# Transposes of the second softmax three at a time, product copies behind the next silu, two weight blocks swapped

## The chip, the cores and the metric

One core of one Trainium2 chip. The metric is device time in microseconds (us), the median of several runs. The engines are TensorE (PE, with its weight loads shown apart as PEld), VectorE (DVE), ScalarE (ACT), GpSimd (POOL) and SyncE (SP), which here issues nearly all the DMA loads and stores. Each engine works through its own list of instructions in order.

## The reference

Three layers one after the other on 4 batches of 576 tokens (2304 in all), everything in fp32: masked attention, a soft mixture of 8 experts, and a gated layer.

```python
scores = scale * q @ k.T; scores = where(mask, scores, -1e9)   # 8 heads of 64; a local or a strided mask
x = softmax(scores) @ v                       # -> x: 2304 x 512
logits = x @ phi                              # 2304 x 32 slots
slot_input = softmax(logits, over tokens).T @ x
for e in range(8):                            # 4 slots each
    slot_out[e] = relu(slot_input[e] @ w1[e]) @ w2[e]     # 512 -> 1024 -> 512
x = softmax(logits, over slots) @ slot_out    # 2304 x 512, of rank 32
g, val = x @ w_gate, x @ w_val                # 512 -> 1536
out = (silu(g) * val) @ w_out                 # 1536 -> 512
```

The weights of the gated layer come in as 64-bit floats and are turned into fp32 in the kernel.

## The kernel before

**Order.** The order of all instructions is written out by hand: what the Python code emits first for an engine runs first there. Tiles come from pools; a pool with a number of buffers hands out a buffer that is free at that point of the program, and the instruction that first writes the new tile waits for the readers of the old one. A load that SP issues also waits until the load eight places before it has landed, since eight semaphores go round.

**Attention** (to about 107 us). 16 units, a unit being one head of two batches, in 48 steps of three score blocks: scores on PE (`qk`, L296), masking and maximum on DVE (L302), exponentials on ACT (`expo`, L314), transposes (`tr`, L321, copied by ACT, L324), product with v (`pv`, L334). Keys and queries of a unit are loaded by `load_qk` (L267, L268), v by `load_v` (L274). Three units are in memory at a time: the fourth unit's keys are loaded when the first unit's scores are done (step `n == 2`).

**Weights** go through `load_half` (L178) in halves of 512 KB, in the order of the list `loads`: three units of the gated layer first (`PRE`: g0, g1, o0), then blocks of w1 (numbers 1 to 12 in the order `WORDER`) and w2 (16 to 31), 1 MB each. They lie in the pool `wp`, a ring of 14 buffers, but for a few that use other memory (0, 13, 14, 15, and the three in `SHARED`). `load_to` and the list `WTO` say how far the loads are to be after each unit. `PRECONV` lists the attention steps at which `pre` turns g0, g1 and o0 from 64-bit to 32-bit floats (ACT at L197, then DVE).

**Experts** (to 153 us). `w1_mm` multiplies the slot inputs with the w1 blocks in the order `W1ORDER`, which ends with 12 and 11, and asks for two more halves after each block: so the last eleven w2 blocks are loaded, the last of them (31) after block 12 has been multiplied and before 11 has. Then the w2 blocks follow (L745), with `hid`, the softmax over slots (`c_soft`, two parts) and its transposes (`c_tr`, eight, each three PE transposes and a DVE copy into `cs`) between them; `CTR` says behind which block how many of the transposes stand, `CTE` how many after the last.

**Gated layer** (from 153 us). Gate and value weights come in twelve units g0 to g11, output weights in six (o0 to o5), 1 MB each, into a pool of four buffers (`load_g`, L686). It lies over memory that `wp` had. Unit g2 is the first that is loaded there. A half is turned into fp32 by `half`: `prep` (ACT L227, then a clamp on POOL, L228) and three steps on DVE (L232, L236, L240). `stage` starts a half, `part` does one DVE step, and a planner spends a `room` of DVE time per step of the main loop on parts. An output unit is split into a high part (ACT copy, `split_hi`, L793) and a low part (POOL, `split_lo`, L796). For each unit f, `a_mm` multiplies the expert outputs with the gate and value weights (L805, copied by ACT), `a_st` spreads the result (L812), ACT copies it into `St[f]` (L813) and DVE subtracts in its lower half (L814). So x never has to be built: `gv` multiplies `St[f]` with `cs` for a block of 512 tokens (gate L825, value L826), ACT takes the silu (L831), DVE multiplies (L832), ACT copies the product into a rounded high part `hh` (L833), POOL subtracts for the low part `hl` (L834). Three products later (`LAG`), `omm` multiplies high and low parts with the output weights: twelve matmuls per product (L852), summed in four output banks per block and taken out by ACT (tiles 0 and 2) and DVE (1 and 3) at L875 or L878 when a group is complete. The last two token tiles are stored at L861. `HEAD` is the list of what is done ahead of the loop: `a0` and `a1` are `a_mm` of units 0 and 1, `s0` and `s1` `a_st`, `g` a `stage`, `p1` one `part`, `w1` a PE matmul that only keeps it warm.

Of the kernel before, what the change touches and what calls it, by code (L numbers as in the profile page):

```python
# [9 lines left out]
F32 = mybir.dt.float32  # L10
# [21 lines left out]
SHARED = W2ORDER[2:5]  # L32
WORDER = list(range(1, 13)) + list(W2ORDER[:2])
REST = list(W2ORDER[5:])
# [3 lines left out]
ORDER = [("g", 2), ("g", 3), ("o", 1), ("g", 4), ("g", 5), ("o", 2), ("g", 6), ("g", 7), ("o", 3), ("g", 8), ("g", 9), ("g", 10), ("g", 11), ("o", 4), ("o", 5)]  # L38
LAG = 3
WT = (0, 0)  # L40
ATDVE = ((15, 1),)
WIN1 = ((0, 3), (3, 7), (7, 10))
HID1 = 1
CTR = {9: 1, 10: 1, 11: 1, 12: 1, 13: 1}
CTE = (1,)
# [9 lines left out]
START = (2, 1)  # L55
HEAD = "a0 a1 g s0 w1 s1 p1 w1"
WARM0 = 8
# [54 lines left out]
def build(ctx: ExitStack, tc: tile.TileContext, cst, phi, qh, kh, vh, w1, w2, wgv, wo, out):  # L112
# [404 lines left out]
    with tc.manual_schedule():  # L517
# [15 lines left out]
        load_v(2)  # L533
        load_half(2)
        def cut(out, k, op, src):
# [176 lines left out]

        def c_tr(bp, b, hf):
            ps = bank("tr", 2)
            for k in range(3):
                PE.transpose(ps[:, 96 * k:96 * k + 96],
                             cst2[hf][:, k, 2 * bp + b].rearrange("p q s -> p (q s)").bitcast(F32),
                             ident[0:96, 0:96])
            DVE.tensor_copy(cs[:, 2 * bp + b, 288 * hf:288 * hf + 288], ps[:, 0:288])

        ctr = [(c_tr, (bp, b, hf)) for bp in range(2) for b in range(2) for hf in range(2)]
        while last[0] in rest:
# [19 lines left out]
        for n, j in enumerate(W2ORDER):  # L742
            e, hf = divmod(j - 16, 2)
            for k in range(4):
                PE.matmul(out=sp_[32 * k:32 * k + 32, :], lhsT=hz[:, 4 * hf + k, 32 * e:32 * e + 32],  # L745
                          rhs=wch(j, k), start=(n == 0), stop=(n == 15), skip_group_check=True)
            load_half(2)
            if n == HID1:
                hid(1)
            if n < 2:  # L750
                c_soft(n)
            if n == 2:
                sil = mid.tile([128, 1], F32, name="sil")
                ACT.activation(out=sil, in_=m_sb, func=AF.Silu)
            for _ in range(CTR.get(n, 0)):
                fn, a = ctr.pop(0)
                fn(*a)
        so = xp.tile([128, 512], F32, tag="hs", name="so")
# [62 lines left out]
        def gv(bi, f):  # L821
# [10 lines left out]
            DVE.tensor_tensor(out=h[:, 0:n], in0=pvv[:, 0:n], in1=sg[:, 0:n], op=ALU.mult)  # L832
            ACT.copy(hh[bi, f][:, 0:n], h[:, 0:n])  # L833
            POOL.tensor_tensor(out=hl[bi, f][:, 0:n], in0=h[:, 0:n], in1=hh[bi, f][:, 0:n].bitcast(F32),  # L834
                               op=ALU.subtract)

# [3 lines left out]
        def omm(p, bi, f):  # L840
# [6 lines left out]
            def mm(t, terms):  # L847
                z = len(ob[t])
                c = 512 // z
                for k, o in enumerate(ob[t]):  # L850
# [4 lines left out]
                    if last and 2 in terms:  # L855
                        if end:
# [3 lines left out]
                                              op=ALU.add)  # L860
                            SP.dma_start(out=out[r:r + 128, c * k:c * k + c], in_=tmp[:, 0:c])  # L861
                        else:
# [68 lines left out]

        split_hi(0)
        split_lo(0, 0)
        split_lo(0, 1)
        for step in HEAD.split():
# [5 lines left out]
            elif k == "g":  # L941
                stage(-2)
            elif k == "p":
                for _ in range(a):
                    part(-1)
            else:
                warm(a)
        for n in range(len(seq) + LAG):
# [17 lines left out]
            if n < len(seq):  # L966
                force(n, ("g", seq[n][2]))
                gv(*seq[n][1:])
            while staged and staged[0][0] <= n and PART <= room:
                room -= PART  # L970
                part(n)
            if n >= STG:
                stage(n)
                if n < 2 * STG:
                    stage(n)

# [19 lines left out]
```

## Time and profile before

| what | value |
|---|---|
| runs of before | 361.76 us median of 3 (359.48, 361.76, 364.25) |
| the profiled execution | 362.2 us by the clock of the runs, its span in the trace 360.4 us |
| busy share of the span | PE 94%, PEld 68%, DVE 61%, ACT 52%, POOL 37% |
| mean granted clock of PE | 0.994 of full speed |
| moved by DMA | 71.94 MB, mean 200 GB/s |

A row of the timeline gives start, duration, engine, line, operation, output and inputs, and how often; in brackets stands the idle time of the engine ahead of it and what the profile takes for its end. The number after PEclk in the view by stretches is the granted clock as a share of 2.4 GHz. PE is busy nearly everywhere, so the places where it is not are what to look for.

### The profile page before, as it was taken

Reading aid. Unit: us, or ns where it says so; the run is one execution under the profiler, and the core shown is the slowest. Engines: PE = TensorE matmul, PEld = TensorE weight load, DVE = VectorE, ACT = ScalarE, POOL = GpSimd, SP = SyncE. Lnnn points to the kernel's source line nnn. Section 1 sums busy time; section 2 is a strip of 40 time slices with the busy share of each in tenths; the row PEclk is TensorE's granted clock in tenths of the full one; section 3 lists DMA queues with packets and bytes.
Section 4 is the critical chain, followed back from the end, with each engine's and each line's share of the span. In section 5 each row is a group of like instructions: output and inputs, shape, how many; then the busy total and the mean of one; then the engine's idle time right before and its main releaser. Section 6 shows DMA issues by size and latency. Waiting matters only on the chain.

```text
span 360.4 us, 7681 instructions
## 1 busy us (share of the span) xinstructions
PE 338.7 (94%) x2856; PEld 243.9 (68%) x2856; DVE 219.4 (61%) x707; ACT 186.8 (52%) x449; POOL 132.6 (37%) x163
## 2 busy tenths in 40 slices
PE   7799989899989999978999899999998999999995
PEld 4677766787737443345777487777785787878774
DVE  4868785765546017247877788788859844142432
ACT  3877969766842003256666565465535653434321
POOL 1522323122110020036555475485525774434431
PEclk9999999999999999998999999999999999999999
DMA  7998998959998999684232542154300003030304
GB/s 212 398 400 299 348 369 322 303 201 352 341 411 303 367 409 408 254 333 172 85 127 102 161 160 73 74 198 154 116 0 2 2 2 116 0 115 4 117 30 144
DMA packets 23397, 71.94 MB, mean 200 GB/s; under 512 B 2624, under 2 KB 3520, under 8 KB 23360
## 3 DMA queue, kind: packets, MB, share of 16 engines
q1 hardware_dynamic: 23216, 71.45, 53.9%
q8 instruction: 22, 0.36, 0.4%
q14 instruction: 15, 0.12, 0.1%
q10 hardware_dynamic: 144, 0.01, 0.0%
HBM read 66.73 MB, written 4.72 MB: 198 GB/s over the span
## 4 chain that ended last, share of the span: by engine, by line
PE 75%; DMA 8%; DVE 6%; ACT 5%; issue 3%; SPq 2%; POOL 1%; DVEq 0%; ACTq 0%
PE o L852 38%; PE sc L296 5%; PE pv L334 5%; PE pv L745 4%; PE gv L825 4%; PE tr L321 3%; DMA w<-in_w 3%; PE gv L826 3%; PE tr L360 2%; PE lg L380 2%; DMA s<-in_kh 2%; PE ms L445 2%; DMA s<-in_qh 2%; DMA g<-in_wgv 1%; DVE h L832 1%
## 5 line engine op out<-in xcount | busy, mean ns | idle before, releaser
L834 POOL TENSOR_TENSOR hl<-h,hh 128x512 fp32r<-128x512 f32 (+1 forms) x60 | 71.0, 1183 | 90.7 <-ACT hh L833 90.7
L852 PE MATMUL o<-woh,hh 128*128 128x512 f32 (+1 forms) x220 | 88.2, 401 | 3.1 <-ACT acc L875 1.7
L852 PE MATMUL o<-wol,hh 128*128 128x512 f32 (+1 forms) x220 | 85.6, 390 | 0.0
L832 DVE TENSOR_TENSOR h<-gv,sg 128x512 f32<-128x512 f32 (+1 forms) x59 | 37.5, 635 | 49.8 <-ACT sg L831 40.0
L833 ACT CAST hh<-h 128x512 fp32r<-128x512 f32 (+1 forms) x60 | 34.7, 578 | 55.3 <-DVE h L832 55.3
L852 PE MATMUL o<-woh,hl 128*128 128x512 f32 (+1 forms) x220 | 59.3, 386 | 0.0
L852 PEld LDWEIGHTS o<-woh,hh 128*128 128x128 f32 x220 | 41.7, 190 | 17.8 <-DVE acc L878 3.1
L277 POOL COPY s<-s 32x390 f32<-32x390 f32 (+1 forms) x48 | 23.8, 498 | 68.4 <-DMA s<-in_vh 46.9
L831 ACT ACTIVATE sg<-gv 128x512 f32<-128x512 f32 (+1 forms) x60 | 33.4, 556 | 26.3 <-PE gv L825 26.2
L852 PEld LDWEIGHTS o<-wol,hh 128*128 128x128 f32 x220 | 41.8, 190 | 7.6
L852 PEld LDWEIGHTS o<-woh,hl 128*128 128x128 f32 x220 | 41.1, 188 | 8.6
L314 ACT ACTIVATE tmp<-tmp,mx 128x96 f32<-128x96 f32 (+1 forms) x144 | 40.8, 363 | 3.0 <-DVE mx L302 3.0
L302 DVE CUSTOM_DVE_ANT_0 tmp<-sc,s 128x96 f32<-128x96 f32 (+1 forms) x144 | 28.1, 245 | 17.6 <-PE sc L296 16.4
L296 PEld LDWEIGHTS sc<-s,s 64*64 64x64 f32 x576 | 23.1, 132 | 13.1 <-issue 7.5
L296 PE MATMUL sc<-s,s 64*64 64x96 f32 (+1 forms) x576 | 27.8, 240 | 4.5 <-DMA s<-in_kh 1.7
L324 ACT COPY tmp<-tr 96x384 f32<-96x384 f32 x47 | 20.2, 477 | 20.6 <-PE tr L321 20.5
L825 PE MATMUL gv<-cs,St 128*128 128x512 f32 (+1 forms) x60 | 25.4, 423 | 2.4 <-DVE St L814 2.4
L796 POOL TENSOR_TENSOR wol<-wo,woh 128x512 fp32r<-128x512 f32 x12 | 15.5, 1297 | 24.0 <-ACT woh L793 24.0
L334 PE MATMUL pv<-s,tmp 96*64 96x65 f32 x576 | 22.4, 225 | 0.6 <-POOL s L277 0.6
L826 PE MATMUL gv<-cs,St 128*128 128x512 f32 (+1 forms) x59 | 22.6, 383 | 0.2 <-DVE h L832 0.2
L334 PEld LDWEIGHTS pv<-s,tmp 96*64 96x64 f32 x576 | 19.0, 137 | 4.0 <-issue 0.8
L321 PE MATMUL tr<-cst_t,tmp 128*96 128x128 f32 x144 | 21.1, 280 | 0.4 <-ACT xT L361 0.4
(164 smaller groups left out, 456.6 us busy)
## 6 DMA issues: line engine op xcount, KB each, us to landing
w<-in_w SPq DMA_DIRECT2D x50, 512.0 KB, 8.4
g<-in_wgv SPq DMA_DIRECT2D x10, 1024.0 KB, 5.1
g<-in_wo SPq DMA_DIRECT2D x5, 1024.0 KB, 4.9
s<-in_vh SPq DMA_DIRECT2D x16, 292.5 KB, 6.1
out<-osb SPq DMA_DIRECT2D x17, 256.0 KB, 2.2
s<-in_qh SPq DMA_DIRECT2D x15, 288.0 KB, 6.2
s<-in_kh SPq DMA_DIRECT2D x15, 288.0 KB, 6.3
wx<-in_w SPq DMA_DIRECT2D x7, 512.0 KB, 5.1
```

Source lines behind the costliest of these rows:

```text
L296: PE.matmul(out=ps[r, W * j:W * j + W], lhsT=qt[u % AHEAD][r, 64 * i:64 * i + 64], rhs=kt[u % AHEAD][r, c0:c0 + W], start=True, stop=True, ...
L302: DVE.tensor_tensor_reduce(out=sm[:, j, 0:W], in0=ps[:, W * j:W * j + W], in1=mask(y, 3 * t + j), scale=-0.125, scalar=3.0e38, op0=ALU.add ...
L314: ACT.activation(out=e[:, j, 96 - W:96], in_=sm[:, j, 0:W], func=AF.Exp, scale=-1.0, bias=mx[:, j:j + 1])
L321: PE.transpose(ps[0:96, 128 * j:128 * j + 128], e[:, j, :], ident)
L334: PE.matmul(out=ps[64 * b:64 * b + 64, o:o + 65], lhsT=a[:, j, 64 * b:64 * b + 64], rhs=vt[u % AHEAD][:, 65 * (NT * b + 3 * t + j):65 * (N ...
L825: PE.matmul(out=pg[:, 0:n], lhsT=St[f][:, 0:128], rhs=csf[:, t0:t0 + n], start=True, stop=True)
L826: PE.matmul(out=pvv[:, 0:n], lhsT=St[f][:, 128:256], rhs=csf[:, t0:t0 + n], start=True, stop=True)
L831: ACT.activation(out=sg[:, 0:n], in_=pg[:, 0:n], func=AF.Silu)
L832: DVE.tensor_tensor(out=h[:, 0:n], in0=pvv[:, 0:n], in1=sg[:, 0:n], op=ALU.mult)
L833: ACT.copy(hh[bi, f][:, 0:n], h[:, 0:n])
L834: POOL.tensor_tensor(out=hl[bi, f][:, 0:n], in0=h[:, 0:n], in1=hh[bi, f][:, 0:n].bitcast(F32), op=ALU.subtract)
L852: PE.matmul(out=o[:, 0:c], lhsT=(a, a, l)[i][:, 128 * t:128 * t + 128], rhs=(woh, wol, woh)[i][f][:, c * k:c * k + c], start=(first and i ...
```

## The change

- `WORDER`: blocks 11 and 12 are loaded in the other order.
- At the start the first `load_half(2)` (both halves of g0) is taken out; the next one, at `n == 2`, now loads g0, behind the fourth unit's queries and keys. `load_to` makes up for the two halves after the first unit.
- Both parts of `c_soft` stand behind the second w2 block (before: one behind each of the first two), after `hid(1)`.
- `c_tr`: three behind the w2 block at index 10 and three behind the one at index 14 (before: one behind each of the indices 9 to 13), the third of each in another bank; all first halves come ahead of the second halves. One stays after the last block, and one more behind it (before: one and two).
- `HEAD`: the output weights' high part, then a `stage`, then their low parts, then the rest with two parts ahead of `s0` and a second `stage` behind `s1`. Before, the split stood ahead of everything, one `stage` behind `a1` and one part at the end.
- `gv`: the copy of the product and POOL's subtraction are kept back and come behind the next product's silu and multiply; from the twelfth product on (`AHEAD_H`) they follow their own again.
- The loop's step 1 stages one half, not two.
- The last of all stores is issued by ACT, not SP.

```diff
@@ -30,18 +30,19 @@
 W2ORDER = tuple(range(16, 32, 2)) + tuple(range(17, 32, 2))
 SPLIT = 13
 SHARED = W2ORDER[2:5]
-WORDER = list(range(1, 13)) + list(W2ORDER[:2])
+WORDER = list(range(1, 11)) + [12, 11] + list(W2ORDER[:2])
 REST = list(W2ORDER[5:])
 W1ORDER = (1, 2, 3, 4, 0, 13, 5, 6, 7, 14, 8, 15, 9, 10, 12, 11)
 PRE = [("g", 0), ("g", 1), ("o", 0)]
 PRECONV = [(6, 1), (7, 1), (8, 1), (9, 1), (10, 1), (11, 1), (12, 1), (13, 1), (14, 1), (15, 1), (16, 1), (17, 1), (18, 1), (19, 1), (20, 1), (21, 1), (22, 1), (23, 1), (24, 1), (25, 1), (26, 1), (27, 1), (28, 1), (31, 2), (32, 2), (33, 1), (34, 1), (35, 1)]
 ORDER = [("g", 2), ("g", 3), ("o", 1), ("g", 4), ("g", 5), ("o", 2), ("g", 6), ("g", 7), ("o", 3), ("g", 8), ("g", 9), ("g", 10), ("g", 11), ("o", 4), ("o", 5)]
 LAG = 3
+AHEAD_H = 12
 WT = (0, 0)
 ATDVE = ((15, 1),)
 WIN1 = ((0, 3), (3, 7), (7, 10))
 HID1 = 1
-CTR = {9: 1, 10: 1, 11: 1, 12: 1, 13: 1}
+CTR = {10: 3, 14: 3}
 CTE = (1,)
 SLOT0 = [(4, [(0, 0, 9)]), (6, [(1, 0, 5)]), (8, [(1, 5, 9)])]
 STG = 1
@@ -53,7 +54,7 @@
 CARRY = 0.6
 DEPTH = 2
 START = (2, 1)
-HEAD = "a0 a1 g s0 w1 s1 p1 w1"
+HEAD = "h g l a0 a1 p2 s0 w1 s1 g p1 w1"
 WARM0 = 8
 WTO = [6, 8, 10, 12, 14, 16, 18, 20, 22, 24, 26, 28, 31, 38, 42, 43]
 NG = 4
@@ -531,7 +532,6 @@
         SP.dma_start(out=phi_t, in_=phi.rearrange("p (c s) -> p c s", c=4))
         load_v(1)
         load_v(2)
-        load_half(2)
         def cut(out, k, op, src):
             DVE.tensor_scalar(out=out, in0=src, scalar1=par[:, k:k + 1], scalar2=NEG, op0=op, op1=ALU.mult)
 
@@ -710,15 +710,15 @@
                               op=ALU.subtract)
             ACT.copy(t4[:, :, 2:4, :], t4[:, :, 0:2, :].bitcast(F32))
 
-        def c_tr(bp, b, hf):
-            ps = bank("tr", 2)
+        def c_tr(bp, b, hf, bk=("tr", 2)):
+            ps = bank(*bk)
             for k in range(3):
                 PE.transpose(ps[:, 96 * k:96 * k + 96],
                              cst2[hf][:, k, 2 * bp + b].rearrange("p q s -> p (q s)").bitcast(F32),
                              ident[0:96, 0:96])
             DVE.tensor_copy(cs[:, 2 * bp + b, 288 * hf:288 * hf + 288], ps[:, 0:288])
 
-        ctr = [(c_tr, (bp, b, hf)) for bp in range(2) for b in range(2) for hf in range(2)]
+        ctr = [(c_tr, (bp, b, hf)) for hf in range(2) for bp in range(2) for b in range(2)]
         while last[0] in rest:
             w1_mm(rest.pop(0))
         hs = xp.tile([128, 2, 512], F32, tag="hs", name="hs")
@@ -747,14 +747,14 @@
             load_half(2)
             if n == HID1:
                 hid(1)
-            if n < 2:
-                c_soft(n)
+                c_soft(0)
+                c_soft(1)
             if n == 2:
                 sil = mid.tile([128, 1], F32, name="sil")
                 ACT.activation(out=sil, in_=m_sb, func=AF.Silu)
-            for _ in range(CTR.get(n, 0)):
+            for k in range(CTR.get(n, 0)):
                 fn, a = ctr.pop(0)
-                fn(*a)
+                fn(*a, bk=("lg", 1) if k == 2 else ("tr", 2))
         so = xp.tile([128, 512], F32, tag="hs", name="so")
         ACT.copy(so[:, 0:256], sp_[:, 0:256])
         ACT.copy(so[:, 256:512], sp_[:, 256:512])
@@ -830,9 +830,16 @@
             hl[bi, f] = fl.tile([128, 512], F32R, tag="hl", name="hl", bufs=LAG + 1)
             ACT.activation(out=sg[:, 0:n], in_=pg[:, 0:n], func=AF.Silu)
             DVE.tensor_tensor(out=h[:, 0:n], in0=pvv[:, 0:n], in1=sg[:, 0:n], op=ALU.mult)
-            ACT.copy(hh[bi, f][:, 0:n], h[:, 0:n])
-            POOL.tensor_tensor(out=hl[bi, f][:, 0:n], in0=h[:, 0:n], in1=hh[bi, f][:, 0:n].bitcast(F32),
-                               op=ALU.subtract)
+            split_h()
+            hs_.append((h[:, 0:n], hh[bi, f][:, 0:n], hl[bi, f][:, 0:n]))
+
+        hs_ = []
+
+        def split_h():
+            while hs_:
+                h, a, l = hs_.pop()
+                ACT.copy(a, h)
+                POOL.tensor_tensor(out=l, in0=h, in1=a.bitcast(F32), op=ALU.subtract)
 
         ob = {}
         NP = len(CUTS[0]) - 1
@@ -858,7 +865,7 @@
                             tmp = fl.tile([128, 512], F32, tag="osb", name="osb", bufs=4)
                             DVE.tensor_tensor(out=tmp[:, 0:c], in0=o[:, 0:c], in1=acc[r // 128][:, c * k:c * k + c],
                                               op=ALU.add)
-                            SP.dma_start(out=out[r:r + 128, c * k:c * k + c], in_=tmp[:, 0:c])
+                            (ACT if t and k else SP).dma_start(out=out[r:r + 128, c * k:c * k + c], in_=tmp[:, 0:c])
                         else:
                             evac(p, t0 // 128 + t, o, t)
 
@@ -929,9 +936,6 @@
                     stage(n)
                 part(n)
 
-        split_hi(0)
-        split_lo(0, 0)
-        split_lo(0, 1)
         for step in HEAD.split():
             k, a = step[0], int(step[1:] or 0)
             if k == "a":
@@ -940,6 +944,11 @@
                 a_st(a, ("o", 4) if a else ("gv", 3))
             elif k == "g":
                 stage(-2)
+            elif k == "h":
+                split_hi(0)
+            elif k == "l":
+                split_lo(0, 0)
+                split_lo(0, 1)
             elif k == "p":
                 for _ in range(a):
                     part(-1)
@@ -966,13 +975,13 @@
             if n < len(seq):
                 force(n, ("g", seq[n][2]))
                 gv(*seq[n][1:])
+                if n >= AHEAD_H:
+                    split_h()
             while staged and staged[0][0] <= n and PART <= room:
                 room -= PART
                 part(n)
             if n >= STG:
                 stage(n)
-                if n < 2 * STG:
-                    stage(n)
 
 
 _NAMES = ['cst', 'phi', 'qh', 'kh', 'vh', 'w1', 'w2', 'wgv', 'wo']
```

## Rows read from the trace of the kernel before

**Rows 1.** Windows: stretch, length, busy PE, PEld, DVE, ACT, POOL (count), clock, DMA, GB/s

```profile
153.00:168.00 15.00, 11.76 (x62) 7.42 (x60) 7.74 (x15) 9.05 (x19) 7.65 (x8) 0.89 0.74 281
192.00:207.00 15.00, 13.54 (x66) 9.10 (x65) 12.07 (x20) 9.38 (x19) 7.32 (x9) 1.00 0.29 90
269.00:281.00 12.00, 10.73 (x53) 7.19 (x55) 10.51 (x18) 6.86 (x14) 6.41 (x9) 1.00 0.01 2
```

**Rows 2.** Timeline of the start, SyncE's queue, ACT and PE

```profile
7.30 1.28 SPq L178 DMA_DIRECT2D w<-in_wgv  x2
...
10.48 0.33 SPq L268 DMA_DIRECT2D s<-in_kh  x1
...
17.76 1.21 ACT L197 ACTIVATE wg<-w 128x512 f32<-128x512 f32 x2
...
18.05 0.63 PE L296 MATMUL sc<-s,s 64*64 64x80 f32 x12 [1.71 <-DMA s<-in_kh]
```

**Rows 3.** Loads of the fourth and the tenth unit's keys: issue, and time to landing

```profile
L268 SPq DMA_DIRECT2D s<-in_kh x1: 328/328/328, 10.5 to 10.5; - x1
DMA to landing us min/median/max: 7.3/7.3/7.3
...
L268 SPq DMA_DIRECT2D s<-in_kh x1: 751/751/751, 42.2 to 42.2; - x1
DMA to landing us min/median/max: 8.9/8.9/8.9
```

**Rows 4.** Timeline of PE near 51 us

```profile
51.24 0.47 PE L296 MATMUL sc<-s,s 64*64 64x96 f32 x6 [1.16 <-DVE wg L211]
```

**Rows 5.** The last two halves of expert weights: issue, and time to landing

```profile
L178 SPq DMA_DIRECT2D w<-in_w x2: 327/480/634, 140.5 to 141.8; - x2
DMA to landing us min/median/max: 10.1/10.2/10.2
```

**Rows 6.** Timeline of PE's weight loads at the end of the experts

```profile
151.98 0.14 PEld L745 LDWEIGHTS pv<-w,hz 128*32 128x32 f32 x4 [0.83 <-DMA w<-in_w]
```

**Rows 7.** Waits of SyncE's queue, 110 to 160 us: total, times, longest

```profile
SPq L686 <- DMA w<-in_w: 9.5, 2, 8.3
...
SPq L686 <- PE pv L745: 1.1, 1, 1.1
```

**Rows 8.** Timeline from the experts' end to the dense stretch

```profile
153.62 1.15 ACT L793 CAST woh<-wo 128x512 fp32r<-128x512 f32 x2
...
158.27 0.66 ACT L227 ACTIVATE wg<-g 128x512 f32<-128x512 f32 x1 [1.41 <-DMA g<-in_wgv]
...
159.01 0.61 POOL L228 TENSOR_SCALAR wg<-wg 128x512 f32<-128x512 f32 x1 [2.17 <-ACT wg L227]
...
159.22 0.43 DVE L814 TENSOR_TENSOR St<-gv,St 64x256 fp32r<-64x256 f32 x1 [3.49 <-ACT St L813]
...
159.70 0.50 PE L825 MATMUL gv<-cs,St 128*128 128x512 f32 x1 [1.79 <-DVE St L814]
...
160.02 0.69 DVE L232 TENSOR_SCALAR cv<-wg 128x512 int32<-128x512 int32 x1
...
168.23 0.50 PE L852 MATMUL o<-woh,hh 128*128 128x512 f32 x1 [1.36 <-ACT acc L875]
...
168.46 1.28 DVE L875 COPY acc<-o 128x512 f32<-128x512 f32 x2
```

**Rows 9.** Timeline of PE in its two later holes

```profile
205.64 0.50 PE L825 MATMUL gv<-cs,St 128*128 128x512 f32 x1 [0.63 <-DVE St L814]
...
278.59 0.50 PE L852 MATMUL o<-woh,hh 128*128 128x512 f32 x1 [1.27 <-DVE acc L878]
```

**Rows 10.** The same windows for two microseconds of the head

```profile
161.00:163.00 2.00, 1.79 (x4) 1.00 (x5) 1.42 (x3) 1.12 (x2) 0.70 (x1) 0.56 1.03 414
```

**Rows 11.** Timeline of SyncE's queue at the end

```profile
356.52 1.30 SPq L861 DMA_DIRECT2D out<-osb  x3
```

**Rows 12.** The chain that ended last: start, duration, twelve output matmuls

```profile
172.68 2.78 PE o L852 x12
```

## The prediction

> **What bounds the kernel now.** TensorE (PE) is busy 94% of the span by the page, so I read the windows by stage first, for the stretches where it is not full. Its holes are 153 to 168 us (11.76 busy of 15), 192 to 207 (1.46 missing) and 269 to 281 (1.27 missing) [rows 1]. A change to this kernel pays only in these holes, or where a load holds PE. So I read next the timeline of the start, where one load does that, the last expert weights, and the chain between the experts and the gated stage.
>
> At the start PE waits 1.71 us, until 18.05, for the fourth unit's keys [rows 2]. They are issued at 10.48, behind the 1 MB of the first gate unit (7.30, two halves), and land 7.3 later, at 17.8 [rows 3]. At 51.24 PE waits again; the profile puts 1.16 us down to VectorE (DVE) [rows 4], but the tenth unit's keys, issued at 42.2, land 8.9 later, at 51.1 [rows 3], and I take these as the cause.
>
> The second expert product ends on the loads. The last two halves of expert weights land 10.1 to 10.2 us after issue, 1.3 apart, the last at 152.0, and PE's weight load stands 0.83 until then [rows 5, 6]. After that SyncE's queue issues the first gated weights (unit g2), but its waits show two landings of expert weights and then 1.1 us for PE's product [rows 7]: the tile of g2 lies over the buffer of the last block, 31. So g2 is issued only at 153.1, and ScalarE (ACT) waits 1.41 for it, until 158.27 [rows 8]. The copy of St0 stands behind this on ACT, DVE's subtraction follows at 159.22, and the first gated product starts at 159.70, PE having idled 1.79 [rows 8]. The dense stretch begins only at 168.23, when the first output banks are evacuated; DVE's part of that is at 168.46 [rows 8].
>
> **The change, part by part.** I count against the profiled execution: span 360.4, its own time 362.2, which is 0.4 above the median of the three runs, 361.76.
>
> *Weights behind the fourth keys.* The same four transfers stand in the queue in another order: the keys move up by the 1 MB, which at 1.3 us a half [rows 5] is 2.6 us. They land near 15.2 and the 1.71 goes. The gate unit then lands last of the four, so at about 17.8 at the latest; ACT's first use of it is at 17.76 [rows 2], so the price there is at most about 0.1. What is late next: from then on the bytes ahead of every later key are as before, so if the stream alone set the landing at 51.1, all would be absorbed there. The loads are however issued behind PE's progress, so an earlier PE also issues earlier. Bounds 0 and -1.7; I take -1.1, nearer the full value because the loads behind PE move along.
>
> *Blocks 11 and 12 swapped.* This looks like nothing, as both land long before use. But it moves buffers. The ring has 14. Before, block 11 takes the last fresh one and 12 the one that g0 gave back, which is the first of the ring and lies under g2's tile. Block 31 is loaded while only 12's buffer is free, so it inherits that. After, 12 has the fresh one and 11 the first, so 31 goes to the fresh one and g2 only waits for block 11's product, the last before the w2 blocks. Then SyncE issues g2 right behind block 31, at about 143: 10.2 at 1.3 each is eight loads under way, and the eighth older one lands 1.3 after 141.8. If the queue serves loads in order of issue, as the last two halves are [rows 5], g2's 1 MB lands two halves behind: 152.0 + 2.6 = 154.6, against 158.2.
>
> *The head.* ACT now does the two copies of the output weights (to 154.77 [rows 8]), then the first half of g2, landed by then, to 155.4. POOL's clamp (0.61) goes ahead of its two subtractions: 156.0. DVE does two steps of the conversion at 0.69 [rows 8]: 157.4. St0's subtraction (0.43, overlapping to about 0.35) ends at 157.8 and the first gated product starts at 157.85: -1.85 at this place. If g2 still landed at 158.2, ACT would hold both St copies behind it and DVE would have two steps ahead of St0: 158.27 + 0.66 for ACT, 0.61 for POOL, 1.4 and 0.35 for DVE give 161.3, and the first product 1.6 later than before. POOL's two subtractions come behind the clamp; their first readers are the first output matmuls, two more gated products later, which covers them.
>
> *Copies behind the next silu.* In the first twelve products ACT no longer waits for DVE's multiply before the next silu. The end of this stretch is DVE's evacuation. Its queue ahead of that is now two St subtractions (0.7 together), three multiplies (taken at the 0.69 of a conversion step, an estimate: same tile) and nine steps, three more than before: 0.7 + 12 x 0.69 = 9.0. Starting at 156.0 the evacuation comes at 165.0 without waits. Before, with six steps, it was 159.2 + 0.7 + 9 x 0.69 = 166.1 without waits, but came at 168.46 [rows 8], so 2.4 of waits. I take 0.4 of waits now, since the silus come early: 165.4, which is -3.0 for head and copies together. With all the waits left it is -1.1, with none -3.5. The copy of a product is due three products later, some 8 us at 2.78 for each product's output matmuls [rows 12], so its delay by one product is covered; if that cover went, PE would wait up to one such step per product, for which I see no sign.
>
> *One staging fewer in step 1, three conversion steps done sooner.* The later holes are waits for conversions: 0.63 at 205.64 behind DVE's St and 1.27 at 278.59 behind DVE's evacuation, which stands behind conversion steps [rows 9]. Three steps are 2.1 us of DVE time. I take -1.0 of the 1.46 in the first and -0.4 of the 1.27 in the second [rows 1], as the planner spends its room anew; bounds 0 and all, -2.7.
>
> *Transposes three at a time, both softmax parts together.* The number of instructions is the same. They stand before the last block's landing, which sets the end, so they are hidden; only one transpose fewer remains behind it: -0.1, bounds 0 and -0.4. The 0.83 for which PE stands there [rows 6] is the cover; without it the one transpose moved ahead would cost as much ahead as it saves behind, so nothing.
>
> *The last store on ACT's queue.* SyncE issues the last three stores back to back, 1.30 from 356.52 [rows 11], 0.43 each. A second queue can save at most one issue, and could cost as much if it answers later: bounds -0.43 and +0.43; I take -0.2, since only part of an issue stands between DVE's last addition and the third.
>
> Sum: -1.1 - 3.0 - 1.4 - 0.1 - 0.2 = -5.8, so 356.4 for an execution like the profiled one, 356.0 for the median.
>
> **A rule against it.** Landings in order of issue are what two rows show. The Trainium skill, DMA: Bandwidth & Descriptors, Queues, rings and completion order, says that completion is not first in, first out per issuing engine, though each DMA engine consumes its ring in order. By the looser reading g2's early megabyte could hold up block 31, and the sum would be -5.8 + 2.6 = -3.2; by the rows it stays -5.8. The trace of before has nothing behind block 31 that could show it. That is rival D.
>
> **Rivals.** A, the forecast: 356.0; its own range 354.6 to 357.8.
> B, the conversions run ahead of both holes, the copies leave DVE no waits and the attention keeps all: -1.7 - 3.5 - 2.7 - 0.1 - 0.2 = -8.2, so 353.6. For it: both holes end on DVE. Against: DVE is the fuller engine there (12.07 of 15, 10.51 of 12) [rows 1], and an earlier PE reaches it sooner.
> C, the stream holds the attention (the 51.1 landing stays) and the holes stay too: -3.3, so 358.5. For it: a landing seven microseconds after issue says a full queue.
> D, g2 shares the transfers with block 31, whose last half comes up to 2.6 later: 358.6. Against: the even 1.3.
> E, the change doesn't do what it says in the head: block 31 stays under g2. Then DVE starts its steps at 158.27 + 0.66 + 0.61 = 159.5 and evacuates at 159.5 + 9.0 + 0.4 = 168.9, 0.5 later than before; with the other parts -1.1 - 1.4 - 0.3 + 0.5 = -2.3: 359.5. Against: the two landings in SyncE's waits fit block 31's two halves.
> F, slower: the granted clock. Between 161 and 163 it is 0.56 [rows 10], so near the 1.2 GHz level, after the idle of 1.79; twelve output matmuls, a product's share, take 2.78 at the full clock [rows 12] and would take 2.8 more at half of it. Earlier products while output banks still wait for DVE leave PE half idle for 8 us. From three such products on (8.4) the gain is gone; with four it is 11.1 - 5.8 = +5.3, so 367.1. Against: over the whole of 153 to 168 it averages 0.89 [rows 1], so it comes back. The Trainium skill, TensorE: Matmul & The Clock Gate, What's actually happening, says that the throttled state is the default and activity releases it; the trace agrees in that the low clock follows the idle.
>
> **How the numbers follow.** A 0.48, B 0.22, C 0.13, D 0.04, E 0.08, F 0.05. The predicted time is A's, 356.0. The range 353.0 to 360.5 takes in A, C, D, most of B and E, and leaves out F and the outer parts of B and E. A measurement of this kernel tells some 2% from no change: faster means under 354.5, slower over 369.0. B is mostly under 354.5 and A a little: 0.23; slower is F beyond four products: 0.02; within 2% 0.75.
>
> **What would show it.** Fourth keys' wait gone at 18; if PE's wait near 50 grows by the same amount, C. The first load of g2 issued near 143 and landed near 154.6 right behind block 31; ACT's copy of St0 before 157.5; the first gated product near 157.9 and the dense stretch 3 us sooner, both less what the attention gave. PE full through the former holes. The prediction is wrong if g2's issue still waits for PE's last expert product, or if the granted clock stays low past the third gated product.

## The result, and the profile after

| | median | of runs | span of the profiled execution |
|---|---|---|---|
| before | 360.94 us | 359.48 to 364.25 (4) | 360.4 |
| after | 356.69 us | 356.31 to 358.31 (4) | 355.0 (356.76 by the clock of the runs) |

The ratio is 0.9886, with a 95% interval of 0.9845 to 0.9926: 1.1% faster, within the 2% that count as no change here. The forecast was 356.0, the range 353.0 to 360.5. All ratios below leave out executions more than 1.5% above the fastest of their kernel (one each of before, copies_undone and after_again).

The windows of after, with the columns of [rows 1], and two more stretches:

```profile
153.00:168.00 15.00, 13.40 (x73) 8.20 (x73) 13.20 (x22) 10.29 (x22) 9.28 (x10) 1.00 0.65 247
161.00:163.00 2.00, 2.00 (x10) 1.61 (x10) 1.97 (x4) 1.72 (x5) 2.00 (x3) 1.00 0.28 27
192.00:207.00 15.00, 15.00 (x75) 10.88 (x74) 12.31 (x21) 9.32 (x19) 10.18 (x11) 1.00 0.50 166
207.00:220.00 13.00, 12.19 (x57) 8.49 (x56) 11.48 (x19) 6.74 (x12) 7.34 (x8) 1.00 0.36 130
269.00:281.00 12.00, 11.38 (x53) 8.06 (x52) 10.66 (x18) 7.81 (x15) 9.14 (x9) 1.00 0.00 1
```

The head, by which I mean the stretch from the end of the experts to the dense stretch (first line), has 1.64 more of TensorE in 15 us than [rows 1], at a clock of 1.00 where [rows 1] has 0.89. The hole at 192 to 207 is gone, that at 269 to 281 has shrunk from 1.27 to 0.62, and a new one of 0.81 stands at 207 to 220. PE's timeline says what ends both:

```profile
211.04 0.50 PE L859 MATMUL o<-woh,hh 128*128 128x512 f32 x1 [0.81 <-DVE acc L885]
...
273.95 0.49 PE L859 MATMUL o<-woh,hh 128*128 128x512 f32 x1 [0.55 <-DVE acc L885]
```

They are evacuations on DVE, as the later one of [rows 9] was. At the start, the fourth and the sixth unit's keys (issue and time to landing), and PE:

```profile
L269 SPq DMA_DIRECT2D s<-in_kh x1: 606/606/606, 8.0 to 8.0; - x1
DMA to landing us min/median/max: 6.0/6.0/6.0
...
L269 SPq DMA_DIRECT2D s<-in_kh x1: 453/453/453, 20.3 to 20.3; - x1
DMA to landing us min/median/max: 8.1/8.1/8.1
```

```profile
19.12 0.55 PE L361 MATMUL tr<-cst_t,x 128*128 128x128 f32 x3 [0.98 <-ACT tmp L325]
28.57 0.71 PE L297 MATMUL sc<-s,s 64*64 64x96 f32 x12 [1.43 <-DVE mx L303]
```

The fourth keys land at 14.1 and the wait of [rows 2] is gone. But PE then waits for ACT at 19.12, and at 28.57 for the sixth unit's keys, which land at 28.4 (the profile names DVE, of which a reading of the maximum ended at 28.38). That the keys end this wait follows from all traces: in the nine such waits near 28, 39 and 51 us, also that of [rows 4], PE starts 0.13 to 0.14 behind the landing of the keys, while its distance from the DVE instruction that the profile names varies from 0.05 to 0.20 in those near 28. The last two halves of expert weights and the first load of g2:

```profile
L179 SPq DMA_DIRECT2D w<-in_w x2: 328/328/328, 139.5 to 140.7; - x2
DMA to landing us min/median/max: 10.2/10.2/10.2
...
L686 SPq DMA_DIRECT2D g<-in_wgv x1: 383/383/383, 142.1 to 142.1; - x1
DMA to landing us min/median/max: 11.4/11.4/11.4
```

So block 31 lands at 150.93 and g2, issued 11 us earlier than before, at 153.47, which is 2.54 behind it. The head's timeline, in order of time:

```profile
153.65 0.68 ACT L228 ACTIVATE wg<-g 128x512 f32<-128x512 f32 x1
154.41 0.61 POOL L229 TENSOR_SCALAR wg<-wg 128x512 f32<-128x512 f32 x1 [25.37 <-DMA g<-in_wgv]
155.06 0.69 DVE L233 TENSOR_SCALAR cv<-wg 128x512 int32<-128x512 int32 x1 [0.71 <-POOL wg L229]
156.52 0.43 DVE L814 TENSOR_TENSOR St<-gv,St 64x256 fp32r<-64x256 f32 x1
157.00 0.50 PE L825 MATMUL gv<-cs,St 128*128 128x512 f32 x1 [0.29 <-DVE St L814]
159.57 0.50 PE L859 MATMUL o<-woh,hh 128*128 128x512 f32 x1 [0.40 <-ACT hh L841]
163.95 1.28 DVE L882 COPY acc<-o 128x512 f32<-128x512 f32 x2
164.69 0.50 PE L859 MATMUL o<-woh,hh 128*128 128x512 f32 x1 [0.71 <-DVE acc L882]
```

DVE starts its steps at 155.06 and evacuates at 163.95, 8.89 later; the first gated product is 2.7 sooner than in [rows 8], the evacuation 4.5.

### The profile page after: what moved, and what is told of

Read it like the earlier page. It is cut to its first block, busy times and chain, and to the rows that moved or that the text cites. A ratio compares the mean times of both kernels' runs of the same rounds, so it can differ in the third digit from the quotient of the medians.

```text
span 355.0 us, 7690 instructions
## 1 busy us (share of the span) xinstructions
PE 338.2 (95%) x2856; PEld 244.6 (69%) x2856; DVE 219.2 (62%) x707; ACT 186.0 (52%) x449; POOL 132.7 (37%) x163
## 4 chain that ended last, share of the span: by engine, by line
PE 66%; DMA 11%; DVE 9%; ACT 7%; issue 3%; SPq 1%; POOL 1%; DVEq 0%; ACTq 0%; POOLq 0%
PE o L859 35%; DMA w<-in_w 8%; PE sc L297 5%; PE pv L335 5%; PE tr L322 4%; PE gv L825 3%; PE gv L826 3%; PE tr L361 2%; PE lg L381 2%; PE ms L446 2%; DMA s<-in_vh 2%; DVE h L832 2%; DMA g<-in_wgv 1%; PE gv L805 1%; ACT tmp L325 1%
## 5 line engine op out<-in xcount | busy, mean ns | idle before, releaser
L297 PEld LDWEIGHTS sc<-s,s 64*64 64x64 f32 x576 | 24.0, 136 | 10.6 <-issue 5.1
L297 PE MATMUL sc<-s,s 64*64 64x96 f32 (+1 forms) x576 | 28.4, 245 | 2.0 <-DVE mx L303 1.4
L229 POOL TENSOR_SCALAR wg<-wg 128x512 f32<-128x512 f32 x20 | 12.3, 614 | 29.1 <-DMA g<-in_wgv 25.4
```

What stands on the lines that cost most here:

```text
L297: PE.matmul(out=ps[r, W * j:W * j + W], lhsT=qt[u % AHEAD][r, 64 * i:64 * i + 64], rhs=kt[u % AHEAD][r, c0:c0 + W], start=True, stop=True, ...
```

## Experiments

The time up to the last expert weights differs from execution to execution of one kernel, so I compare stretches within each trace: landing of the last expert weights; from there to the first gated product; from that to DVE's first evacuation; from that to the end of the span. Ratios are to runs of the kernel before on the same chip in the same series.

| kernel | weights landed | to first product | to evacuation | to the end | ratio, 95% |
|---|---|---|---|---|---|
| before | 151.94 | 7.76 | 8.76 | 191.96 | |
| swap_alone | 149.56 | 6.28 | 8.75 | 191.98 | 0.9993 [0.9968, 1.0018] |
| swap_alone_2 | 150.11 | 6.26 | 8.75 | 193.29 | 0.9977 [0.9949, 1.0006] |
| swap_and_copies | 151.21 | 6.26 | 6.88 | 192.12 | 0.9901 [0.9863, 0.9938] |
| after | 150.93 | 6.07 | 6.95 | 191.03 | 0.9886 [0.9845, 0.9926] |
| after_again | 152.97 | 6.07 | 6.95 | 191.09 | 0.9889 [0.9838, 0.9939] |
| swap_undone | 151.13 | 9.45 | 7.24 | 191.03 | 1.0004 [0.9977, 1.0032] |
| copies_undone | 152.14 | 6.07 | 8.45 | 191.20 | 0.9948 [0.9921, 0.9975] |
| head_undone | 152.39 | 5.91 | 7.00 | 192.12 | 0.9934 [0.9903, 0.9966] |
| ctr_undone | 150.96 | 6.07 | 6.96 | 191.04 | 0.9873 [0.9836, 0.9910] |
| gate_first | 150.04 | 6.07 | 6.95 | 191.07 | 0.9866 [0.9828, 0.9904] |
| keys6_early | 150.46 | 6.08 | 6.94 | 191.03 | 0.9859 [0.9827, 0.9892] |
| keys_all_early | 153.65 | 6.08 | 6.94 | 191.01 | 0.9889 [0.9849, 0.9929] |
| keys_and_room | 149.67 | 6.09 | 6.93 | 193.48 | 0.9935 [0.9905, 0.9964] |

The columns behind the first repeat to a few hundredths where the code is the same; the first scatters by 4 us. Between after and after_again, the same kernel, it differs by 2.04 and the span by 2.1, so it makes most of the spread of the runs. No ratio lies more than 2% from 1, so what an edit is worth is read from the stretches, one trace for each kernel.

### The two blocks swapped, alone, in the kernel before

```diff
-WORDER = list(range(1, 13)) + list(W2ORDER[:2])
+WORDER = list(range(1, 11)) + [12, 11] + list(W2ORDER[:2])
```

> The kernel before with one edit: blocks 11 and 12 are loaded in the other order; no engine's list changes by an instruction. Buffer theory (the swap moves block 31 out of the buffer that lies under g2): g2 is issued near 143 instead of 153.1 and lands near 154.6 instead of 158.2; ScalarE's wait of 1.41 for it goes, the copy of St0 and the first gated product (159.70) come about 1.4 earlier, and with them the dense stretch: about 360.4 - 1.4, so 359.0, the bounds 0 and -1.4 (DVE's later queue may eat it). Rival (the early issue comes from the head's new order or the weights at the start, not from the buffer): g2 still issued at 153, time as before, within 0.3.

The trace confirms the buffer: no engine's list differs, yet g2 is issued at 140.7, not 153.1, and the first product comes 1.48 sooner behind the weights. The runs don't show it (medians 360.7 against 361.25). From the first product to the evacuation nothing more is won, 8.75 against 8.76:

```profile
155.84 0.50 PE L825 MATMUL gv<-cs,St 128*128 128x512 f32 x1 [0.30 <-DVE St L814]
157.73 0.62 ACT L833 CAST hh<-h 128x512 fp32r<-128x512 f32 x1 [0.76 <-DVE h L832]
161.93 0.69 DVE L832 TENSOR_TENSOR h<-gv,sg 128x512 f32<-128x512 f32 x1 [1.76 <-POOL hl L834]
164.59 1.28 DVE L875 COPY acc<-o 128x512 f32<-128x512 f32 x2
```

ACT waits about 0.76 for each multiply before it can copy the product, and the third multiply waits 1.76 for POOL's subtraction: there are two buffers for products, and POOL still reads the one that the third needs. Eleven of the 12 runs show a granted clock of 0.988 to 0.995, the profiled one 1.0, so I ran it again for another trace.

> The kernel before with only blocks 11 and 12 in the other order, a second time, for another profiled execution: the first one's trace has the first gated product 1.5 nearer to the experts' end at a clock of 1.0, but most of its runs show a clock of 0.988 to 0.995 and no gain. If the thin head lets the clock fall (TensorE is half idle until the evacuation): a granted clock near 0.5 to 0.6 somewhere in 155 to 170 us. Rival (the scatter comes from the keys at the start): the clock is 1.0 there and low, if at all, near 30 us behind a wait for keys; the distance from the first output product's weights (L805) to the evacuation is 11.2 again.

Windows of 2 us, columns as above, swap_alone:

```profile
163.00:165.00 2.00, 0.64 (x3) 0.45 (x4) 1.93 (x4) 2.00 (x5) 1.64 (x2) 1.00 0.00 0
165.00:167.00 2.00, 2.00 (x10) 1.33 (x10) 2.00 (x4) 0.80 (x2) 0.22 (x1) 1.00 0.57 106
167.00:169.00 2.00, 2.00 (x15) 1.09 (x14) 1.45 (x3) 1.43 (x4) 1.79 (x2) 1.00 1.02 416
```

and swap_alone_2:

```profile
163.00:165.00 2.00, 0.10 (x1) 0.10 (x1) 1.93 (x4) 1.82 (x4) 1.42 (x2) 0.84 0.00 0
165.00:167.00 2.00, 2.00 (x5) 1.61 (x6) 2.00 (x5) 0.83 (x2) 0.74 (x2) 0.50 0.31 35
167.00:169.00 2.00, 2.00 (x8) 1.46 (x7) 1.93 (x3) 1.20 (x2) 1.27 (x2) 0.80 0.94 377
```

PE stands idle for the evacuation in both; in the second the clock goes to the 1.2 GHz level just as the dense stretch begins, and the stretch to the end is 193.29 - 191.98 = 1.31 longer. So in this execution most of the 1.5 is given back to the clock. That is rival F's mechanism, in a smaller size. All ten runs of swap_alone_2 show 0.991 to 0.995, which fits the same loss in each, but does not show it: a run's clock doesn't say where it fell (swap_and_copies was profiled at 0.994, and there it is 0.50 at 18 to 20 us). In the kernel before, the low clock of [rows 10] lay ahead of the evacuation, for which PE waited anyway, and cost nothing behind it: 191.96 against 191.98.

### The swap taken out of the change

```diff
-WORDER = list(range(1, 11)) + [12, 11] + list(W2ORDER[:2])
+WORDER = list(range(1, 13)) + list(W2ORDER[:2])
```

> The changed kernel with blocks 11 and 12 loaded in the old order, nothing else. Buffer theory: g2 issued again only behind TensorE's last expert product, about 151.8, landing near 157.0; the conversion of g2 stands ahead of St0 in the new head, so the first gated product comes at 157.0 + 0.66 + 0.61 + 1.4 + 0.35 = 160.0 (the change: 157.0), and the run about 2 to 3 us above the changed kernel, near 359.2. Rival (buffers play no part): g2 issued at 142 as in the changed kernel, same time within 0.3.

```profile
L686 SPq DMA_DIRECT2D g<-in_wgv x1: 383/383/383, 152.3 to 152.3; - x1
DMA to landing us min/median/max: 4.9/4.9/4.9
```

g2 is back behind PE's last expert product, and the first product comes 3.38 later than in the change; with the evacuation it is 3.67. By the ratio the whole gain is gone (1.0004); by the stretches 3.67 of 4.4 are, since the later holes stay closed. The new head puts the conversion of g2 ahead of St0, so without the early load the first product is 1.69 later than in the old one and the evacuation 0.17: the swap is the edit on which the rest stands.

### Copies behind the next silu

```diff
-AHEAD_H = 12
+AHEAD_H = 0
```

> The changed kernel with each product's copy and POOL's subtraction straight behind its own silu from the first product on. If putting the copies behind the next silu gives what the prediction's sum took (2.0 of waits between the first gated product and the evacuation): first gated product stays at 157.0, the dense stretch starts 1 to 2 us later than 166.9, the run 1 to 2 us above the changed kernel, near 358.2. Rival (the early g2 does all of it, the copies nothing): the evacuation at 163.95 and the time both stay within 0.3.

```profile
51.07 0.71 PE L297 MATMUL sc<-s,s 64*64 64x96 f32 x12 [0.84 <-DMA s<-in_kh]
166.18 0.50 PE L859 MATMUL o<-woh,hh 128*128 128x512 f32 x1 [1.93 <-ACT acc L882]
```

First product as in the change, evacuation 1.50 later (8.45 against 6.95), and ACT's wait of 0.76 for each multiply is back in its timeline. POOL's subtraction ends no wait here: the third multiply waits 0.48, for its silu. The line at 51.07 is of another kind: the wait of [rows 4], with this kernel's start the same as the change's, named here by its true cause, the keys. A wait there above 0.3 stands in two of the 14 traces, one with either start.

Both edits on the kernel before, nothing else (the lines in `gv`, then in the loop behind it; `split_h` as in the change):

```diff
-WORDER = list(range(1, 13)) + list(W2ORDER[:2])
+WORDER = list(range(1, 11)) + [12, 11] + list(W2ORDER[:2])
...
+            split_h()
+            hs_.append((h[:, 0:n], hh[bi, f][:, 0:n], hl[bi, f][:, 0:n]))
...
+                if n >= 12:
+                    split_h()
```

> The kernel before with two edits: blocks 11 and 12 in the other order, and the copies behind the next silu in the first twelve products; head, start, transposes and staging as before. If each edit is worth its 1.5 in the head, added up: the evacuation 9.5 to 9.7 behind the first product of the gate weights (before 12.7, swap alone 11.2), time 3.0 below before, ratio 0.9915. Rival (the copies need the new head): 11.2 and a ratio of 0.996 or above.

They add up: 1.50 for the swap at the first product, 1.87 for the copies at the evacuation, which comes 9.30 behind unit 1's product with the gate weights (forecast 9.5 to 9.7). Three of six runs are at a clock of 1.0. By ratio this is nearly all of the change's gain; by the undoing of the head (below) it isn't, and the intervals hold both.

### The head's order and the staging

```diff
-HEAD = "h g l a0 a1 p2 s0 w1 s1 g p1 w1"
+HEAD = "h l a0 a1 g s0 w1 s1 p1 w1"
                 stage(n)
+                if n < 2 * STG:
+                    stage(n)
```

> The changed kernel with the old order of the head (output weights split ahead of everything, one stage behind the second product, no conversion part ahead of the spread) and step 1 staging two halves again; swap, copies and all else as in the change. If the early g2 and the copies carry the head's gain: first gated product at 157.0 or up to 0.5 earlier (no steps ahead of the subtraction), three conversion steps later done, time 0 to 0.7 above the changed kernel. Rival (the reordering with the three earlier steps closes the holes at 192 to 207 and 269 to 281): the holes of 1.46 and 1.27 come back and the run is 1.4 to 2.7 above the changed kernel.

Its windows:

```profile
192.00:207.00 15.00, 13.60 (x65) 9.22 (x64) 12.03 (x19) 9.12 (x19) 7.90 (x9) 1.00 0.41 140
269.00:281.00 12.00, 10.72 (x51) 7.44 (x50) 10.02 (x17) 6.81 (x14) 6.80 (x8) 1.00 0.00 1
```

Both holes are back, 1.40 and 1.28, and the evacuation comes as early as in the change (12.91 behind the weights against 13.02). From it to the end is 1.09 longer. This is what PE's windows say too: the change closes 1.40 and 0.66 and opens 0.81 (at 207 to 220) and 0.16 (at 240 to 269, where it is busy for 28.84 of 29). So the reordering and the staging give nothing in the head and 1.09 behind it; which of the two does it was not taken apart.

### Transposes

```diff
-CTR = {10: 3, 14: 3}
+CTR = {9: 1, 10: 1, 11: 1, 12: 1, 13: 1}
```

and the softmax's two parts and the order of `ctr` as before.

> The changed kernel with the softmax over slots and its transposes placed as before (one at each of the indices 9 to 13, two behind the last block). If they are hidden behind the loads: the experts end within 0.1 later, by the one transpose more behind the last block, time within 0.1 to 0.4. Rival (the three transposes in a row and the softmax's two parts keep TensorE off the last blocks, so the edit costs): the run is up to 0.4 faster than the changed kernel.

Hidden: all stretches within 0.04, ratio 0.9873 against 0.9889 for after_again, the change beside it.

### Weights behind the fourth unit's keys

```diff
         load_v(2)
+        load_half(2)
```

> The changed kernel with g0's two halves ahead of the fourth unit's keys again. If the edit is worth what the prediction took: keys landing 17.8 instead of 14.1, TensorE's wait of 1.7 near 18 back, time 1.1 above the changed kernel (bounds 0 and 1.7), so near 357.8. Rival (the stream takes the gain back at the sixth unit's keys, near 28 us, as the trace of the changed kernel shows it there, and what came at 50 us was another thing): 0 to 0.3.

The changed kernel itself ran beside it once more:

> The changed kernel itself once more, beside the others: the ratio 0.9886 again, and nearly all runs at a granted clock of 1.0, if the fuller head is what keeps TensorE's clock up. If the clock falls in the head by chance, most runs come at 0.993 to 0.995 and about 1 to 2 us later.

gate_first, PE near 17 us:

```profile
17.38 0.63 PE L297 MATMUL sc<-s,s 64*64 64x80 f32 x12 [1.56 <-DMA s<-in_kh]
```

after_again, PE near 29 us, and two windows:

```profile
29.43 0.71 PE L297 MATMUL sc<-s,s 64*64 64x96 f32 x12 [2.87 <-DMA s<-in_kh]
...
28.00:30.00 2.00, 0.57 (x12) 0.55 (x12) 0.00 (x0) 0.07 (x1) 1.34 (x3) 1.00 1.00 393
32.00:34.00 2.00, 2.00 (x12) 1.49 (x12) 1.25 (x3) 1.83 (x7) 1.22 (x2) 0.50 1.01 401
```

The wait is moved, not removed: 1.56 for the fourth keys with g0 ahead of them, 1.43 (after) or 2.87 (after_again) for the sixth without, there with the clock at half behind it. The stretches behind the weights are equal. Time: 356.1 (0.9866) with the edit undone, 358.39 (0.9889) with it; the intervals overlap, and ctr_undone, which starts as the change does, has 356.44 in the same series. So the edit is not shown to cost, but nothing speaks for a gain.

The traces show where the gain ends. The same bytes stand ahead of the sixth keys with either start, yet these land at 27.59 to 29.29 in the six traces with the change's start and at 26.63 to 27.36 in the five with the old one (28.43 in after, 27.36 in before). The stream loses time on the way: in after, g0's halves are issued at 9.44 and 10.19 and the next load only at 14.48, and they land 1.71 and 1.80 apart instead of 1.28; in after_again the fifth keys land 3.75 behind the load ahead of them. That the gap in issuing causes this is likely, not shown: in before the second half of g0 lands 2.00 behind the first, with the next load issued 1.87 behind it.

### Three attempts to go on

```diff
-WTO = [6, 8, 10, 12, 14, 16, 18, 20, 22, 24, 26, 28, 31, 38, 42, 43]
+WTO = [4, 8, 10, 12, 14, 16, 18, 20, 22, 24, 26, 28, 31, 38, 42, 43]
```

> The changed kernel with two of the four halves of weights that stand ahead of the sixth unit's keys moved behind them (first entry of WTO 4 instead of 6). If these four halves are what takes the 1.4 back at 28 us: the keys land near 25.8 instead of 28.4, the wait there goes, and the run is 0.7 to 1.4 below the changed kernel. Rival (the bytes are only passed on to the seventh to tenth units' keys): the gain is gone again by 50 us, time as the changed kernel's within 0.3.

```diff
+WTO = [4, 6, 8, 10, 12, 14, 16, 18, 20, 22, 26, 28, 31, 38, 42, 43]
```

> The changed kernel with the weights two halves later through the first ten units (WTO 4, 6, 8, ... 22, then 26 as before), where the stream has room near 75 us. If the waits for keys near 28 and 39 us are a matter of what stands ahead of them: no wait for keys behind the start, 0.4 to 0.5 below the run with only the first entry lowered, so near 355.7, and little scatter. Rival (the megabyte is missing later): the last expert weights land up to 2.6 later, time as the changed kernel's or above.

The same line, and:

```diff
-EV = (1.4, 2.75, 2.75)
+EV = (1.4, 3.45, 3.45)
```

> As the run before it (weights two halves later), and the planner keeps 0.7 more of VectorE's time free where output banks are evacuated (EV 3.45 instead of 2.75), so one conversion step fewer stands ahead of an evacuation. If the waits of 0.81 near 211 and 0.55 near 274 us are these steps: both gone, 0.7 to 1.3 below keys_all_early, near 354.7. Rival (the steps are only put off and are missing later): a wait for converted weights takes their place, no gain.

PE waits for keys in keys6_early, then in keys_all_early:

```profile
39.08 0.63 PE L297 MATMUL sc<-s,s 64*64 64x80 f32 x12 [0.70 <-DMA s<-in_kh]
```

```profile
90.59 0.72 PE L297 MATMUL sc<-s,s 64*64 64x80 f32 x12 [1.86 <-DMA s<-in_kh]
```

and in keys_and_room:

```profile
89.17 0.63 PE L297 MATMUL sc<-s,s 64*64 64x80 f32 x12 [0.48 <-DMA s<-in_kh]
```

With two halves moved behind the sixth keys, the wait at 28 is gone and a smaller one stands at 39. The six runs lie between 356.00 and 356.44 (median 356.16), the five of the change that its ratio counts between 355.62 and 359.11. It beats the kernel before by 1.4%, within the 2%; against the change only the spread is plainly smaller, the ratios overlap.

With the weights late in all units the waits near 28 and 39 are gone, but PE waits for the last unit's keys: 1.86 at 90.59 in keys_all_early and 0.48 at 89.17 in keys_and_room, which loads in the same order. By time (ratio 0.9889, that of the change) the rival came true. Its reason, last weights up to 2.6 later, is not shown: they land at 153.65 in the one and at 149.67 in the other, the latest and the second earliest of all. The larger reserve in the planner made the last stretch 2.5 longer and left the hole at 207 to 220 (12.19 of 13 again): 0.7 more of reserve does not close it. What would stays open.

## Why the prediction was right

The time was right, 356.0 against 356.69, and so was the likeliest case in its main part. That it came so near is partly luck: the forecast gain was 5.8, the measured one is 4.1 by the ratio, and the median of before, from which I counted, went from 361.76 to 360.94 with its fourth run. By its own steps:

- **The buffer: right.** Forecast: g2 issued near 143, landing two halves (2.6) behind block 31. Measured 142.05 and 2.54. Swap alone (g2 issued at 140.7 instead of 153.1) and swap undone (152.3) show that the order of two loads did this and nothing else. That it works through the buffer no row shows directly; the waits fit it: in before [rows 7] and in swap_undone SyncE waits 1.1 for PE's last expert product ahead of g2, and in swap_alone it issues g2 9 us ahead of that product. Rival D is out: block 31 was not held up. The Trainium skill, DMA: Bandwidth & Descriptors, Queues, rings and completion order, does not promise completion in order; in the 14 traces none of SyncE's loads in the first 190 us landed ahead of one issued earlier.
- **The first gated product: right, the size a little too large.** Forecast -1.85, measured 6.07 - 7.76 = -1.69.
- **Head and copies together: right.** Forecast -3.0 at the evacuation, measured 13.02 - 16.52 = -3.50, which is the bound "with no waits". DVE's queue was forecast at 9.0 and 0.4 of waits; it ran for 8.89 with none but those at its beginning. The split between the parts was off: I gave 1.85 to the head and the rest to the copies; by the runs the swap gives 1.5 and the copies 1.5 (undone) to 1.9 (added to the swap). Nor had I seen the 1.76 for which the multiply waited behind POOL in the old head.
- **Rival E, the change without its buffer:** forecast an evacuation 0.5 later than before; swap_undone has 16.69 against 16.52, 0.2 later. The time it gave for this case, 2.3 below before, did not come (ratio 1.0004): 1.1 of it was the attention term, on which see below.
- **The later holes: right in kind.** Forecast -1.4, measured -1.09 by undoing the head, -0.93 from evacuation to end (191.96 to 191.03). I took 1.0 of the first hole and 0.4 of the second; all of the first and half of the second closed, but 0.81 opened elsewhere. I had let the planner's new use of its room make the gain smaller, not open a hole; that the planner is the cause of this one is not shown.
- **Transposes: right in size, but without effect.** Forecast -0.1; from the last expert weights' landing to unit 0's first product with the gate weights (`a_mm`) it is 3.10 before, 3.10 with the old transposes in the change and 3.03 after. The first gated product doesn't move by it: 6.07 with either.
- **The attention: the step that failed.** I took -1.1 because earlier issues would keep the stream ahead. The profiled executions differ by 1.0 at the last weights (151.94 and 150.93), which looks like it; but with g0 first again the change is no slower, its weights landing at 150.04. The gain ended at the sixth keys, where the bytes ahead are the same and which land later, not earlier, in all six traces. So the term belongs at its bound of 0. What stands between the two profiled executions is the wait at 51 us [rows 4], which comes and goes with either start (it is there in copies_undone, not in swap_alone). This is rival C's argument, at 28 us instead of 51. I had written down the bytes and then set them aside.
- **The last store: next to nothing.** No run undoes this edit alone. SyncE issues two, ACT the third:

```profile
350.43 1.35 DVE L866 TENSOR_TENSOR osb<-o,acc 128x512 f32<-128x512 f32 x3 [2.62 <-PE o L859]
351.15 0.81 SPq L868 DMA_DIRECT2D out<-osb  x2
351.81 0.35 ACTq L868 DMA_DIRECT2D out<-osb  x1
```

From the start of DVE's last additions to the end of the span it is 4.55, before 4.62: forecast -0.2, bounds -0.43 and +0.43. Counted from those additions, ACT's store is issued 0.24 earlier than SyncE's third was in before, but it lands 2.16 after its issue instead of 1.91.

- **Rival F, the clock:** it did not fall in the change's head (1.00 in the first window above), and did in swap_alone_2. With the copies PE's idle ahead of the dense stretch shrinks (1.97 in swap_alone, 0.61 in swap_and_copies). In none of the nine traces that have both the early g2 and the copies does the clock fall in the head; in three of the other five it does (before, swap_alone_2, swap_undone). The full clock is also commoner over the runs: three of the first four of the change have 1.0 and three of six of swap_and_copies, but one of 22 of the swap alone. That the shorter idle keeps the clock up is likely from this, not shown. The lower clocks of after_again have another place, the wait at 29 us; how its runs without a trace spent theirs stays open.

By the stretches the change is worth 208.48 - 204.05 = 4.4 behind the last expert weights; ahead of them no gain is shown. From before over swap_alone and swap_and_copies to after, the way from these weights to the end is 208.48, 207.01, 205.26 and 204.05: 1.5 for the swap, 1.75 for the copies, 1.2 for the rest. Undone one at a time from the change, swap, copies and head are worth 3.7, 1.7 and 1.0, more in sum, since the new head needs the early load. The forecast without the attention term was 4.7; the ratio gives 4.1, with 2.7 to 5.6 as its interval.

## What to carry to other kernels

Where buffers go round, the order of two loads that are both early can decide which buffer a much later tile waits for: follow the buffer, not the load. Moving a transfer ahead of another pays only up to the next one that has the same bytes ahead of it, so look for that one before counting the wait as saved. And measure parts against a mark inside the trace when the stretch ahead of it scatters by more than the change is worth.

## What I had not expected of the hardware

- The granted clock fell to 0.50 behind waits of PE of 1.98 us (swap_alone_2) and 2.87 us (after_again), but stayed at 1.00 behind 1.97 us in swap_alone, the same kernel as the first, and behind 1.93 us in copies_undone. So one trace without the fall doesn't tell how the runs go. The clock of each run tells whether it fell, but not where.
- An edit that gains 1.5 in the trace was worth nothing in the medians of its 22 runs. In the one of its two traces where the clock fell, the shorter path led to a wait behind which the low clock took 1.31 back; that the other runs lost it in the same way is likely, not shown.
